# Gated linear attention and a maxout feed-forward on one core: an explicit list of steps for every engine in place of woven generators

## The chip, the core and the metric

The kernel runs on one core of one Trainium2 chip. A core has a matrix engine (TensorE, PE in the profile; its weight loads are counted apart as PEld), VectorE (DVE), ScalarE (ACT), GpSimd (POOL) and SyncE (SP), which here only starts transfers between HBM and the on-chip memory. Each engine works through its own queue in order and waits on semaphores for the others. The metric is the device time of one execution in microseconds; lower is better. A profiled span, from the first to the last instruction, is about 1 us shorter than the time.

## What is computed

The reference is a gated linear recurrence with a complex decay, followed by a feed-forward layer whose hidden value is the greatest of three products.

```python
# attention: B, H, S, D = 4, 8, 768, 48; q, k, v, a_re, a_im of that shape
mag   = sqrt(a_re**2 + a_im**2)
scale = minimum(mag, 0.999) / (mag + 1e-6)
a     = (a_re + 1j * a_im) * scale
for t in range(S):
    state = a[:, :, t, :, None] * state + k[:, :, t, :, None] * v[:, :, t, None, :]
    y[:, :, t] = q[:, :, t] @ state.real
# feed-forward: 3072 tokens, 384 channels, 768 hidden
x   = y, heads side by side           # (3072, 384)
h   = maximum(maximum(x @ w1, x @ w2), x @ w3)
out = h @ w_out
```

## The kernel before

The recurrence is done in chunks. A **tile** is 128 steps of one batch entry with all 8 heads; a **group** is a pair of tiles (two batch entries, called x and y here), and there are 12 groups. Everything is float32. For one group the work is this:

- **Gates** (the pair at once, 128 x 768): logarithm and angle of the decay, by a chain of ScalarE functions and VectorE sums. `Ln` holds minus the logarithm of the magnitude, `w` the angle in turns.
- **Sums**: TensorE adds `Ln` along time (`sums`); ScalarE takes exponentials `E` and `En`, with which key and query are multiplied. TensorE also adds the angles (`cs`), ScalarE takes sine and cosine (`CS`).
- **Tile steps**: `uk`, `uq` (key and query times sine and cosine), transposed by TensorE (`tp`) and copied by ScalarE to `K` and `Q`; decay factors between sub-chunks (`F` on TensorE, four exponentials `f` on ScalarE), with which VectorE makes further copies of query and key (three products into `Q`, and `KB`, `QB`, `QG`); scores `A` and `B` on TensorE, collected into `atm` by masked copies; state update (`dk` on TensorE, four operations on `g` by VectorE); output `y`, copied to `xT`.
- **Feed-forward**: six `up` blocks per group (18 matmul records each, 768 columns of PSUM) copied or maximised into `hT`, and one `op` block per tile, copied to `ot` and sent out.

All blocks of TensorE take their PSUM room from one pool of four buffers, in the order in which the program asks for them:

```python
psum = ctx.enter_context(tc.tile_pool(name="psum", bufs=4, space=PSUM))
def banks(nm, n=None):
    ps = psum.tile([P, 2, 512], FP, tag="ps", name=nm)
```

The weights come in as pairs of 32-bit words and are turned to float32 on the chip, in 12 blocks, each by two ScalarE and four VectorE instructions of 128 x 768:

```python
nc.scalar.activation(out=ex.bitcast(FP), in_=high.bitcast(FP), func=AF.Abs)                    # a
nc.vector.tensor_scalar(out=ex.bitcast(FP), ..., op0=OP.max, op1=OP.min)                       # b
nc.vector.tensor_single_scalar(out=ex, in_=ex, scalar=3, op=OP.logical_shift_left)             # c
nc.scalar.activation(out=dst, in_=low, func=AF.Copy, scale=2.0 ** -51, bias=2.0)               # d
nc.vector.tensor_tensor(out=ex, in0=ex, in1=dst.bitcast(I32), op=OP.add)                       # e
nc.vector.scalar_tensor_tensor(out=dst.bitcast(I32), in0=high, ..., in1=ex, ...)               # f
```

The decays of key and query, and the squares of the gates:

```python
for nm, sg in (("k", 1.0), ("q", -1.0)):
    E = nat2.tile([P, DM], FP, tag="E", name="E")
    act(out=E..., in_=ps[:, :, 0:HC], func=AF.Exp, scale=sg)
    eng = nc.gpsimd if g > 1 else nc.vector
    eng.tensor_tensor(out=hd(T[nm, x]), in0=E, in1=hd(T[nm, x]), op=OP.mult)
...
nc.scalar.activation(out=w, in_=ar, func=AF.Square)
nc.scalar.activation(out=L, in_=ai, func=AF.Square)
nc.vector._custom_dve(dve_ops.TENSOR_ADD_SAT, out=L, in0=L, in1=w, s0=LARGE, s1=SMALL)
```

The order of the program: group 0 is written out, with the weight blocks put in by hand and by `weave`, which merges several lists of steps by fractions of a common length. Groups 1 to 11 are run by `group(g)`. The program's framework may move instructions within an engine's queue as long as the data allows it. Bound are only ScalarE's functions (`tab`, because of the table loads between exponentials and sines) and, from group 2 on, TensorE's order (`chained`).

```python
weave((0.0, 1.0, tile_steps(0) + tile_steps(1)), (0.0, 0.7, rounds), (0.15, 0.58, pre_steps(1)),
      (0.415, 0.44, ffn[:6]), (0.55, 0.75, ffn[6:9]), ...)
def group(g):
    ...
    if g > 1: feed(1)                 # feed(n): the next n feed-forward blocks of the group before
    pairs(x)                          # scores A and B of tile x, and their collection
    if g > 1: gates[2]()              # last part of the gates of group g + 1
    feed(1)
    ...
    turned(y)                         # transposes, F and state of x, first query factors of y
    sums[0](); sums[1]()
    feed(1); outputs(x, tokens(x)); rest(y)
    turning()                         # angles of group g + 1; feed(2) inside
    pairs(y); ...; feed(2); turned(y + 1)
    feed(1); outputs(y, tokens(y)); rest(y + 1)
    feed(len(ffn))
for g in range(1, NG):
    if g == 2: T["chain"] = None      # TensorE's order is bound from here on
    group(g)
```

## Time and profile before

| | |
|---|---|
| time, median of 3 | 667.58 us (667.13 to 668.19) |
| profiled span | 666.7 us |
| TensorE busy | 581.8 us, 87% |
| VectorE busy | 476.9 us, 72% |
| ScalarE busy | 404.2 us, 61% |
| GpSimd busy | 122.4 us, 18% |
| TensorE clock granted, mean | 0.963 |
| instructions | 22,815 |

The page gives for every engine the time in which at least one of its instructions ran. A group line names the source line, the engine and operation, the output and inputs with their shapes and the count; after the bar stand the busy time, the mean duration of one, and the idle time of the engine just before it with what ended that idle time. Records of one engine overlap a little[...], so the step from start to start is shorter than the duration: a 128 x 768 VectorE operation shows 0.95 us and follows the last one by 0.87 us. Nearly all matmuls have the source line of one helper, so they are told apart by their tiles (`up`, `op`, `y`, `A` and so on).

### The profile page before, as it was taken

The page shows a single profiled execution, that of the slowest core. Times are in us where ns is not written, and L with a number is a line of the kernel's source. Part 1 is how long each engine was busy: PE and PEld are TensorE (multiplying, and loading weights), DVE is VectorE, ACT ScalarE, POOL GpSimd, SP SyncE. Part 2 cuts the span into 40 slices and gives each one's busy share as a digit, 9 for nine tenths or more (in the row PEclk, how much of TensorE's full clock was granted, in tenths as well). Part 3 has the DMA queues.
Part 4 walks back from the last instruction along what each step waited for, and adds up shares of the span by engine and source line. Part 5 has one row for each costly group of instructions (what it writes and reads, how often), then busy time and mean ns, then how long its engine had stood idle before and what let it go on. Part 6 is the DMA issues. An engine that isn't in the chain of part 4 may idle for free.

```text
span 666.7 us, 22815 instructions
## 1 busy us (share of the span) xinstructions
PE 581.8 (87%) x10076; PEld 472.5 (71%) x10076; DVE 476.9 (72%) x638; ACT 404.2 (61%) x670; POOL 122.4 (18%) x131
## 2 busy tenths in 40 slices
PE   1244777898999999999999999999999999999997
PEld 0143665777877878868868867878878777878785
DVE  3899998985777877877776687778778777655111
ACT  6889696577476567567566665765764854631000
POOL 9400102305113114013014013023023023000000
PEclk9956898997999999999999999999999999999999
DMA  6975542330330330330330420421320210000000
GB/s 134 272 166 142 139 83 56 62 62 14 61 65 24 61 69 19 65 69 15 73 61 15 83 52 24 76 53 35 67 56 15 40 47 3 2 27 2 19 7 24
DMA packets 136547, 39.26 MB, mean 59 GB/s; under 512 B 129152, under 2 KB 132224, under 8 KB 136448
## 3 DMA queue, kind: packets, MB, share of 16 engines
q1 hardware_dynamic: 136448, 37.80, 26.1%
q8 instruction: 79, 1.29, 0.8%
q14 instruction: 20, 0.16, 0.1%
HBM read 33.03 MB, written 4.72 MB: 57 GB/s over the span
## 4 chain that ended last, share of the span: by engine, by line
PE 46%; ACT 24%; DVE 16%; issue 8%; DMA 3%; SPq 2%; POOL 1%; DVEq 0%; POOLq 0%; ACTq 0%
PE up L117 24%; PE op L117 12%; DVE Q L533 6%; PE y L117 3%; ACT CS L112 3%; ACT f L112 2%; ACT L133 2%; ACT e L112 2%; PE A L117 2%; ACT Q L505 2%; PE cs L117 2%; ACT K L501 2%; PE dk L117 2%; DVE g L632 2%; DMA ai<-in_a_im_dram 1%
## 5 line engine op out<-in xcount | busy, mean ns | idle before, releaser
L117 PE MATMUL up<-xT,w 128*128 128x256 f32 (+1 forms) x1404 | 295.9, 369 | 11.0 <-ACT f L112 4.5
L117 PEld LDWEIGHTS up<-xT,w 128*128 128x128 f32 x1404 | 249.0, 192 | 46.9 <-ACT f L112 7.7
L533 DVE TENSOR_TENSOR Q<-Q,f 112x512 f32<-112x512 f32 (+2 forms) x72 | 91.6, 1278 | 49.2 <-ACT f L112 49.2
L117 PE MATMUL op<-wo,hT 128*128 128x384 f32 x288 | 99.0, 494 | 0.5 <-ACT K L501 0.4
L117 PEld LDWEIGHTS op<-wo,hT 128*128 128x128 f32 x288 | 53.2, 190 | 34.9 <-DVE hT L676 0.8
L674 ACT COPY hT<-up 128x768 f32<-128x768 f32 (+2 forms) x27 | 19.6, 727 | 91.8 <-PE up L117 91.7
L676 DVE TENSOR_TENSOR hT<-hT,up 128x768 f32<-128x768 f32 (+2 forms) x54 | 46.4, 859 | 38.8 <-PE up L117 38.7
L381 POOL TENSOR_TENSOR ai<-ai,L 128x768 f32<-128x768 f32 x10 | 22.3, 2226 | 276.9 <-ACT L L112 188.0
L117 PE MATMUL A<-Q,K 112*32 112x80 f32 x1536 | 34.7, 247 | 12.8 <-DVE Q L533 12.8
L117 PEld LDWEIGHTS A<-Q,K 112*32 112x32 f32 x1536 | 29.9, 117 | 21.8 <-issue 13.6
L117 PE MATMUL y<-atm,vb 128*32 128x64 f32 x1152 | 39.5, 224 | 0.9 <-issue 0.7
L117 PEld LDWEIGHTS y<-atm,vb 128*32 128x32 f32 x1152 | 32.6, 112 | 10.4 <-issue 5.6
L112 ACT ACTIVATE f<-F 48x280 f32<-48x280 f32 x96 | 38.3, 399 | 0.9
L117 PE MATMUL y<-QG,g 112*32 112x64 f32 x1408 | 38.3, 220 | 0.0
L487 DVE TENSOR_TENSOR uk<-uk,En 128x768 f32<-128x768 f32 x24 | 24.5, 1021 | 18.0 <-PE tp L117 18.0
L477 POOL TENSOR_TENSOR k<-E,k 128x384 f32<-128x384 f32 x20 | 25.6, 1279 | 63.7 <-ACT E L112 63.7
L389 POOL TENSOR_TENSOR ai<-ai,carry 1x768 f32<-1x768 f32 x10 | 18.6, 1864 | 92.8 <-ACT ai L386 92.8
L117 PE MATMUL sums<-Ln,mid 64*64 64x192 f32 x192 | 15.8, 378 | 22.7 <-DVE Ln L371 22.7
L117 PEld LDWEIGHTS y<-QG,g 112*32 112x32 f32 x1408 | 34.9, 110 | 0.4 <-ACT g L630 0.2
L477 POOL TENSOR_TENSOR q<-E,q 128x384 f32<-128x384 f32 x20 | 34.9, 1747 | 0.0
L117 PE MATMUL cs<-w,upto 128*64 128x192 f32 x192 | 20.1, 355 | 15.7 <-DVE w L400 15.7
L412 DVE SCALAR_TENSOR_TENSOR nf<-t,cs 128x384 f32<-128x384 f32 x24 | 13.3, 554 | 28.5 <-ACT t L410 27.4
(103 smaller groups left out, 949.9 us busy)
## 6 DMA issues: line engine op xcount, KB each, us to landing
ar<-in_a_re_dram SPq DMA_DIRECT2D x24, 192.0 KB
ai<-in_a_im_dram SPq DMA_DIRECT2D x24, 192.0 KB
k<-in_k_dram SPq DMA_DIRECT2D x96, 48.0 KB
q<-in_q_dram SPq DMA_DIRECT2D x96, 48.0 KB
vb<-in_v_dram SPq DMA_DIRECT2D x96, 48.0 KB
out_dram<-ot SPq DMA_DIRECT2D x24, 192.0 KB
raw<-in_moe_w_dram SPq DMA_DIRECT2D x5, 768.0 KB
w<-in_moe_w_dram SPq DMA_DIRECT2D x2, 768.0 KB
```

Source lines behind the costliest of these rows:

```text
L112: tab(nc.scalar.activation(**kw))
L117: ins = f(**kw)
L133: tab(nc.scalar.preload_act_table_set(nm))
L381: (nc.gpsimd if g > 1 else nc.vector).tensor_tensor(out=ai, in0=ai, in1=L, op=OP.mult)
L389: nc.gpsimd.tensor_tensor(out=ai[0:1], in0=ai[0:1], in1=T["carry", g], op=OP.subtract)
L477: eng.tensor_tensor(out=hd(T[nm, x]), in0=E, in1=hd(T[nm, x]), op=OP.mult)
L487: nc.vector.tensor_tensor(out=u, in0=u, in1=two(T["En", x]), op=OP.mult)
L501: nc.scalar.copy(out=T["K", x][0:DD].rearrange("p n (j t) -> p j n t", j=2), in_=src)
L505: nc.scalar.copy(out=T["Q", x][0:DD, :, 0:32].rearrange("p (n j a) t -> p j n a t", n=H, j=2), in_=src.rearrange("p j n (a t) -> p j n a t ...
L533: nc.vector.tensor_tensor(out=out, in0=in_, in1=f.to_broadcast([DD, 2 * H - g, n, 8]), op=OP.mult)
L674: nc.scalar.copy(out=dst, in_=ps)
L676: nc.vector.tensor_tensor(out=dst, in0=dst, in1=ps, op=OP.max)
```

## The change

All work is cut into single steps of about one instruction (one TensorE block, one ScalarE function, one transfer), and their order is written down in two lists. `SCHEDULE` has 472 steps: groups 0 and 1 with their weights, the feed-forward of group 0, and the first half of group 2. `CYCLE` has 143 steps and is run for g from 2 to 13: it finishes tile work of group g, prepares group g + 1, does the six `up` blocks of group g - 1 and the `op` blocks of groups g - 2 and g - 1. Every instruction of every engine is bound to the one before it, so each queue has exactly the order of the lists. It is meant to let TensorE's blocks, their emptying and the weights be placed step by step.

```diff
-    mm, mt = chained(nc.tensor.matmul), chained(nc.tensor.transpose)
+    class Bound:
+        def __getattr__(self, name):
+            f = getattr(self.engine, name)
+            def g(*a, **kw):
+                ins = f(*a, **kw)
+                if self.last is not None:
+                    tc.add_manual_dep(ins.ins, self.last.ins.name, order, reason="the schedule's order")
+                self.last = ins
+                return ins
+            return g
+    pe, dve, act, pool, sp = (Bound(e) for e in (nc.tensor, nc.vector, nc.scalar, nc.gpsimd, nc.sync))
...
-                eng = nc.gpsimd if g > 1 else nc.vector
-                eng.tensor_tensor(out=hd(T[nm, x]), in0=E, in1=hd(T[nm, x]), op=OP.mult)
+        elif name in ("mk", "mq"):
+            t = hd(T[name[1], x])
+            dve.tensor_tensor(out=t, in0=T["E" + name[1], x], in1=t, op=OP.mult)
...
-            nc.scalar.activation(out=w, in_=ar, func=AF.Square)
+            activation(out=e, in_=ar, func=AF.Square)
...
-    weave((0.0, 1.0, tile_steps(0) + tile_steps(1)), (0.0, 0.7, rounds), (0.15, 0.58, pre_steps(1)), ...)
-    for g in range(1, NG):
-        if g == 2:
-            T["chain"] = None
-        group(g)
+    program(SCHEDULE, 0)
+    for g in range(2, NG + 2):
+        program(CYCLE, g)
```

Table loads are now put in wherever the next function needs the other set, by the order of the list. The square of `a_re` goes to `e` in place of `w`. In the lists a name ends in the tile (x or y) and, after the colon, the group; `U01` is the `up` block of the first half of the hidden channels with the second weight, `u01` its maximum or copy, `O` and `o` the `op` block and its copy, `W` the weight steps a to f above, `L` a load, `D` a store. TensorE's part of `CYCLE`:

```
U00:-1 tpky:0 tpqy:0 Fy:0 U10:-1 Ax:0 Bx:0 Ox:-2 sumsx:1 sumsy:1 dkx:0 U11:-1 U01:-1 U02:-1
csy:1 csx:1 yx:0 Ay:0 By:0 U12:-1 dky:0 Fx:1 Oy:-1 yy:0 tpqx:1 tpkx:1
```

and the same stretch of VectorE's and ScalarE's part, from the first block to the second scores:

```
VectorE: mqy:0 uqy:0 Q1x:0 Q2x:0 Q3x:0 Lnop:1 KBx:0 QBx:0 addw:1 g0x:0 g1x:0 g2x:0 g3x:0 kEny:0 kEnx:0
         mkx:1 mulw:1 h0x:0 stt:1 mky:1 h1x:0 QGx:0 Q2y:0 u11:-1 h2x:0 QBy:0 mulr:1 addi:1 h3x:0
         u01:-1 Q1y:0 Q3y:0 u02:-1 nfy:1 KBy:0 ...
ScalarE: Qcx:0 expw:1 Kcx:0 relu:1 u00:-1 Kcy:0 Qcy:0 lne:1 f0y:0 f3y:0 f2y:0 abs:1 f1y:0 u10:-1 lnw:1
         b0x:0 expL:1 b1x:0 ox:-2 Ekx:1 sign:1 Eky:1 Eqx:1 Enx:1 cpai:1 Eqy:1 cpar:1 Eny:1 atan:1 ty:1
         tx:1 sby:1 afx:1 sbx:1 sax:1 xx:0 ...
```

## The prediction

> **What bounds the kernel now.** I began with the busy times in three stretches: the start, up to 151 us (where the fourth tile's output has just been copied to `xT`, at 144.85, and the second tile's result to `ot`, at 148.08), then the regular middle, then the tail. Columns after the stretch: its length, then busy us and instruction counts of TensorE, its weight loads, VectorE, ScalarE, GpSimd, the clock, DMA share, GB/s.

> ```profile
> 0.00:151.00 151.00, 86.08 (x1830) 72.42 (x1831) 128.53 (x201) 115.92 (x191) 34.42 (x78) 0.86 0.54 124
> 151.00:580.31 429.31, 413.36 (x7305) 335.30 (x7303) 322.40 (x401) 274.47 (x454) 88.00 (x53) 0.99 0.22 45
> 580.31:662.70 82.39, 82.39 (x944) 64.80 (x944) 25.99 (x36) 13.35 (x27) 0.00 (x0) 1.00 0.04 14
> 662.70:666.70 4.00, 0.01 (x1) 0.00 (x0) 0.00 (x0) 0.48 (x1) 0.00 (x0) 0.88 0.14 51
> ```

> TensorE has 581.8 us of work in a span of 666.7. Its idle time is 151.00 - 86.08 = 64.9 us in the start, 429.31 - 413.36 = 16.0 us in the middle, none in the tail, and 4.0 us at the very end (last copy and store). The start is VectorE's: 128.53 of 151 us, 85%, with ScalarE at 77%. The middle and tail are TensorE's.

> Next the middle by group. Two whole groups, same columns:

> ```profile
> 191.82:240.76 48.94, 47.21 (x853) 38.18 (x853) 37.48 (x48) 31.61 (x53) 9.89 (x6) 1.00 0.25 51
> 434.38:483.33 48.95, 47.22 (x854) 38.19 (x853) 37.49 (x48) 31.62 (x53) 9.88 (x6) 1.00 0.26 51
> ```

> A group takes 48.9 us, of which TensorE works 47.2. (Groups that lack some matmul records show less, so I take these two.) What ends its 1.7 us of idling is in the waits of TensorE between 175 and 575 us: waited for, total us, times, longest:

> ```profile
> PE dk L117 <- DVE hT L676: 5.5, 8, 0.7
> PE up L117 <- ACT f L112: 3.9, 8, 0.6
> PE up L117 <- DVE g L633: 3.6, 6, 0.6
> PE op L117 <- ACT K L501: 0.4, 1, 0.4
> ```

> None of these is data the block needs: `dk` doesn't read `hT`, and `up` reads neither `f` nor `g`. They are the four PSUM buffers: a block waits until the fourth block before it has been emptied. So 13.4 us in all are lost to late emptying.

> Last, VectorE beside GpSimd. Instructions in time order (start, duration): the query factor operations of 112 x 1024 and 112 x 768 while GpSimd rests, and then while it multiplies keys and queries:

> ```profile
> 144.10 1.22 DVE L533 TENSOR_TENSOR Q<-Q,f 112x1024 f32<-112x1024 f32 x1
> 145.70 0.95 DVE L533 TENSOR_TENSOR Q<-Q,f 112x768 f32<-112x768 f32 x1
> ...
> 162.92 1.97 DVE L533 TENSOR_TENSOR Q<-Q,f 112x1024 f32<-112x1024 f32 x1
> 164.81 1.35 DVE L632 TENSOR_TENSOR g<-g,f 112x384 f32<-112x384 f32 x1
> 166.08 1.74 DVE L533 TENSOR_TENSOR Q<-Q,f 112x768 f32<-112x768 f32 x1
> ```

> ```profile
> 163.77 1.98 POOL L477 TENSOR_TENSOR q<-E,q 128x384 f32<-128x384 f32 x1
> 165.71 1.30 POOL L477 TENSOR_TENSOR k<-E,k 128x384 f32<-128x384 f32 x1
> ```

> The same operation takes 0.95 us alone and 1.74 us beside GpSimd's products.

> [...] The trace has 25 loads of mean 1283 ns. [...]

> **The change part by part.**

> *Decays to VectorE.* From group 2 on, 4 products of 128 x 384 per group leave GpSimd (two of 1.2 us and two of 1.8 us) and come to VectorE at 0.47 us from start to start: +1.9 us per group. Against that the stretched operations return to their free length. Summing VectorE's 51 steps of `CYCLE` at free durations (14 of 0.47, 15 of 0.87, 4 maxima of 0.86, 4 of 1.13, 6 of 0.61, 2 of 0.62, 6 of 0.34) gives 34.5 us per group, against 37.5 now. VectorE has ample room in a group of 47 us; so has ScalarE, 30.0 us plus two table loads, 32.6. In the middle this part alone is worth almost nothing; its use is that the emptying comes on time.

> *The cycle.* I laid TensorE's blocks of `CYCLE` end to end (`up` 4.06 each, `op` 4.1, `y` 1.73, `A` 1.2, `dk` 1.1, others 0.5 to 0.8) and asked at each block when the fourth one before is emptied and when its data are there, going through the other two orders at free durations. Examples, in us from the start of `U00`: `U10` begins at 5.6 and needs `U00` copied, done 4.9. `Ax` (9.7) needs Q3x, done by 4.1. `sumsy` (16.4) needs A's masked copies, 12.8. `U01` (22.4) needs the three exponentials of `sumsx`, 19.3. `csy` (30.5) needs the angles, 26.7, the latest chain of gates, through GpSimd's product and carry. `Ay` (33.7) needs the maximum u02, 31.4. `yy` (45.3) needs QGy, 42.8. The next `U00` (48.1 in this sum) needs the copy of `yy`, about 47.8: two transposes of 1.1 us in all cover it. Every block has its condition ahead of time, most by over 2 us. So I expect at most 0.2 us of idling per group against 1.7: a period near 47.3 us.

> *The start.* Loads of the 472 steps at free durations: VectorE 111.6 us (weights alone 12 x (0.47 + 0.47 + 0.87 + 0.87) = 32 us) plus 3 us of memsets; TensorE 72 us; ScalarE 104.2 us plus 11 table loads by the list's alternations (1 first, 10 changes) of 1.28 = 14.1, so 118.3. Before had 7 loads up to 151 us. ScalarE is now the longest queue. It also starts late: in the chain of waits the first weight block lands at 11.2 us (3.69 + 7.53) and its first step follows, when ScalarE has done only about 6.4 us of the gates; this 4.9 us remains. The last ScalarE step needed for `yy:1`, the fourth tile's output, is at 101.4 + 10 x 1.28 of its queue, which puts the end of the list on TensorE at no earlier than 4.9 + 114.2 + 1.7 + 1.1 = 122 us. VectorE's bound is close to it (106.6 before `yy:1`, after about 10 us of waiting for the first data: 117, plus 2.8 for the last blocks). Two queues of nearly equal length that feed each other won't be without gaps. With ScalarE at 93% instead of 97% of that stretch the end is at about 128 us. That is my choice; the one stretch before ran at 77 to 85%.

> *What is left after the list.* Ten cycles of 47.2 are 472; the first lacks one `op` (-4.1), the last lacks the preparation of a next group (sums 1.6, cs 1.5, transposes 1.1, F 0.6: -4.8); then six `up` of group 11 (24.4) and three `op` (12.4): together 500 us. Before, TensorE has 413.4 + 82.4 = 495.8 us left at 151 us: the same work within its missing records, so the list's end stands for that 151.

> *Sum.* 128 + 500 + 10 x 0.2 + 0.7 (the last copy of `yy`, which no transposes cover) + 4.0 (end) + 0.9 (time over span, 667.6 - 666.7) = 635.6. I say 636 us.

> **Rivals.** (a) *The start gains nothing*: more table loads and a fixed order, in which one late transfer holds a whole queue. For it: DMA is busy 78% in the first 50 us, the weight blocks follow each other closely in the list, and SyncE's order is bound as well. Against it: the loads are written well ahead of their use in the list. Then the list ends at 151 and the time is about 659, within 2%. (b) *The cycle gets a new wait every time*, say for the angles through GpSimd or for `xT` at the seam. At 1.7 us each it would be 15 us more than I say, about 651. Against it: the slack above. (c) *VectorE becomes the bound* with 4 more products: it would need 47 us; even at its present stretched 37.5 + 1.9 = 39.4 it wouldn't be. (d) *The start is packed almost fully*, the list ends at 122: 630.

> **Range and chances.** The start is uncertain by some 7 us to either side, more to the slow side, the cycle by 0 to 8 in all, TensorE's work by 3 (clock in the start, 0.69 between 25 and 50 us, and missing records). Range 625 to 652. Over 2% faster means below 654.2, which only a failed start or a wait in every cycle would prevent: 0.90. Within 2%: 0.08. Slower: 0.02.

> **What would show it.** Right: regular periods of 47.2 to 47.5 us with TensorE waits under 0.3 us; the `xT` copy of the fourth tile at about 126 us in place of 144.85; ScalarE over 90% busy in the first 128 us, with 11 table loads; 112 x 768 query factors at a mean of 0.95 to 1.0 us in place of 1.67; only gate product and carry on GpSimd. Wrong: a wait of over 0.5 us that returns every period, or queue gaps in the start behind transfers or behind each other that put the fourth tile past 140 us.

## The result, and the profile after

The changed kernel takes 645.67 us (645.16 to 646.76, four runs) against 667.88 us (667.13 to 668.80) for the kernel before on the same chip: 0.967 of the time, with a 95% interval of 0.965 to 0.969. The profiled span went from 666.7 to 645.1 us. The prediction was 636 us in a range of 625 to 652: inside the range, and 9.7 us too low. This part follows those 9.7 us. The profiled run took 646.76 us, the slowest of the four, so its trace is some 1.1 us longer than the median run.

The stretches of the kernel after, cut where the list ends on TensorE (137.1 us) and where TensorE ends (641.5 us). Columns as in the prediction: length, busy us and counts of TensorE, weight loads, VectorE, ScalarE, GpSimd, then clock, DMA share, GB/s.

```profile
0.00:137.10 137.10, 83.38 (x1729) 70.28 (x1729) 115.56 (x193) 114.17 (x188) 31.82 (x74) 0.93 0.53 127
137.10:641.50 504.40, 495.68 (x8350) 403.02 (x8348) 359.99 (x488) 295.69 (x487) 43.34 (x17) 1.00 0.21 43
641.50:645.10 3.60, 0.01 (x1) 0.00 (x0) 0.00 (x0) 0.48 (x1) 0.00 (x0) 0.80 0.15 55
```

The opening ends at 137.1 in place of 151.0: 13.9 us gained. What is left after it takes 504.4 in place of 662.7 - 151.0 = 511.7: 7.3 us gained. The last copy and store give 0.4. So two thirds of the gain are the opening, one third is the cycle, and both were to give more.

TensorE's waits from 140 to 640 us (waited for, total us, times, longest):

```profile
PE B L129 <- issue: 4.1, 4, 1.4
PE dk L129 <- issue: 2.1, 1, 2.1
PE A L129 <- issue: 1.9, 2, 1.1
PE up L129 <- ACT xT L129: 0.6, 1, 0.6
```

The three waits for PSUM buffers that came back in every group are gone altogether. In their place stand eight single stops, 8.7 us in all; seven of them are put down to `issue`, which means that the profile shows nothing that TensorE waited for. A cycle without a stop, in the same columns, has no idle time on TensorE:

```profile
372.70:419.54 46.84, 46.84 (x856) 38.26 (x858) 37.59 (x53) 31.77 (x52) 5.99 (x2) 1.00 0.27 53
```

From copy to copy of the second tile's output the cycle takes 46.83 us in three groups and 47.5 to 48.3 us where there is a stop; it was 48.94. Group 6 takes 45.92: the two tiles there begin new batch entries (768 steps are six tiles), so half of its `y` products with a state fall away, 64 records in place of 128.

Now the opening, in steps of 25 us:

```profile
0.00:25.00 25.00, 3.15 (x80) 2.65 (x80) 12.37 (x35) 17.38 (x32) 22.03 (x71) 1.00 1.01 244
...
25.00:50.00 25.00, 8.80 (x128) 6.32 (x128) 24.15 (x37) 24.46 (x40) 0.48 (x2) 1.00 0.52 135
50.00:75.00 25.00, 15.51 (x285) 13.84 (x279) 25.00 (x37) 23.96 (x39) 2.40 (x1) 0.73 0.53 135
75.00:100.00 25.00, 21.61 (x409) 19.93 (x407) 23.29 (x37) 22.05 (x35) 6.90 (x2) 0.93 0.25 61
100.00:125.00 25.00, 24.27 (x408) 18.86 (x412) 24.09 (x39) 19.52 (x32) 0.00 (x0) 1.00 0.42 78
```

The third busy number is VectorE's: 96.5 of the 100 us after the first 25. VectorE is closer to full than ScalarE (90.0), so I take it to be what sets this stretch; but in the first 25 us it works for 12.4. The largest single cause, in the timelines of ScalarE, VectorE and GpSimd (start, duration, instruction, in brackets the idle time before it and its releaser):

```profile
19.25 0.40 ACT L129 ACTIVATE f<-F 48x280 f32<-48x280 f32 x1 [4.43 <-POOL maskf L129]
```

```profile
21.27 0.58 DVE L129 TENSOR_SCALAR ex<-ex 128x768 f32<-128x768 f32 x1 [4.35 <-ACT ex L129]
```

```profile
8.79 9.42 POOL L129 TENSOR_SCALAR_AFFINE_SELECT cuts<-cuts 64x4 f32<-64x4 f32 x32
```

GpSimd is still making the constants `cuts` until 18.2 us. The matrix `F` needs them, the first exponential `f` needs `F`, and ScalarE stands at that exponential for 4.4 us, because its queue is bound, although the next weight step `ex` (step a) needs nothing of it. VectorE waits for that `ex`. Releasers are inferred; the chain through `F` is in the code, and an experiment below undoes it.

### The profile page after: what moved, and what is told of

It reads as the page before. It is cut to its first block, busy times and chain, and to the rows that moved or that the text cites. A ratio compares the mean times of both kernels' runs of the same rounds, so it can differ in the third digit from the quotient of the medians.

```text
span 645.1 us, 22666 instructions
## 1 busy us (share of the span) xinstructions
PE 579.1 (90%) x10076; PEld 473.3 (73%) x10076; DVE 475.6 (74%) x680; ACT 410.3 (64%) x676; POOL 75.2 (12%) x91
## 3 DMA queue, kind: packets, MB, share of 16 engines
q8 instruction: 79, 1.29, 0.9%
## 4 chain that ended last, share of the span: by engine, by line
PE 82%; issue 8%; POOL 4%; ACT 2%; DMA 1%; DVE 1%; SPq 1%; POOLq 0%; ACTq 0%; DVEq 0%
PE up L129 42%; PE op L129 15%; PE y L129 6%; PE A L129 4%; PE tp L129 4%; PE dk L129 3%; PE sums L129 2%; PE cs L129 2%; PE B L129 2%; PE F L129 1%; POOL cuts L129 1%; DMA raw<-in_moe_w_dram 1%; POOL ai L129 1%; SPq L129 1%; POOL maskf L129 1%
## 5 line engine op out<-in xcount | busy, mean ns | idle before, releaser
L129 DVE TENSOR_TENSOR hT<-hT,up 128x768 f32<-128x768 f32 (+1 forms) x56 | 46.8, 836 | 52.7 <-PE up L129 52.7
L129 DVE TENSOR_TENSOR Q<-Q,f 112x512 f32<-112x512 f32 (+2 forms) x72 | 75.9, 1067 | 4.9 <-ACT Q L129 4.2
L129 ACT ACTIVATE t<-cs 128x384 f32<-128x384 f32 x24 | 11.8, 491 | 59.5 <-PE cs L129 59.5
L129 PEld LDWEIGHTS y<-atm,vb 128*32 128x32 f32 x1152 | 33.9, 114 | 17.7 <-issue 17.4
L129 PE MATMUL y<-QG,g 112*32 112x64 f32 x1408 | 39.4, 223 | 0.0
L129 ACT ACT_TABLE_LOAD x30 | 38.5, 1283 | 1.2 <-PEq L781 0.8
L129 ACT COPY ot<-op 128x384 f32<-128x384 f32 x24 | 11.5, 480 | 43.5 <-PE op L129 36.0
L129 DVE SCALAR_TENSOR_TENSOR Ln<-L,e 128x768 f32<-128x768 f32 (+1 forms) x13 | 11.7, 897 | 37.2 <-ACT e L129 36.5
L129 POOL TENSOR_TENSOR ai<-ai,carry 1x768 f32<-1x768 f32 x10 | 28.4, 2837 | 70.9 <-ACT ai L129 70.9
L129 ACT COPY atm<-B 32x256 f32<-32x256 f32 x48 | 17.3, 361 | 28.5 <-DVE atm L129 25.8
L129 ACT COPY hT<-up 128x768 f32<-128x768 f32 (+1 forms) x28 | 19.8, 708 | 23.1 <-PE up L129 20.7
L129 DVE COPY_PREDICATED atm<-maskd,A 128x512 f32<-128x512 uint8 x24 | 17.6, 734 | 22.0 <-PE A L129 22.0
```

Of the source, the lines that this page charges most:

```text
L129: ins = f(*a, **kw)
```

## The experiments

"4th `xT`" is the start of the copy of the fourth tile's output, near the list's end; "3rd" is that of the tile before. The regular cycle is the usual distance from the copy of one second tile's output to the next. Times are medians, and each ratio is to the kernel before on the same chip, with its 95% interval. Differences between two changed kernels are taken from their ratios, times 667.6 us.

| | time, us | ratio | 3rd, 4th `xT`, us | regular cycle, us |
|---|---|---|---|---|
| before | 667.88 | 1 | 123.6, 144.8 | 48.94 |
| after | 645.67 | 0.967 (0.965 to 0.969) | 127.7, 136.1 | 46.83 |
| e1_before_decay_dve | 663.18 | 0.994 (0.992 to 0.996) | 124.4, 144.7 | 48.28 |
| e2_after_decay_pool | 657.45 | 0.986 (0.983 to 0.988) | 128.1, 136.4 | 48.8 |
| e3_free_vector_pool_sync | 664.31 | 0.996 (0.994 to 0.997) | 128.3, 136.7 | 48.9 |
| e4_f_later | 642.99 | 0.964 (0.961 to 0.967) | 125.2, 133.4 | 46.83 |
| e5_v_early | 646.49 | 0.968 (0.967 to 0.970) | 128.0, 134.5 | 46.83 |
| e6_gate_product_dve | 642.72 | 0.963 (0.962 to 0.965) | 127.1, 133.6 | 46.83 |
| e7_up_between | 657.33 | 0.985 (0.983 to 0.986) | 127.1, 134.5 | 48.73 |
| e8_all | 656.32 | 0.983 (0.982 to 0.985) | 124.8, 132.1 | 48.73 |
| e9_opening | 642.07 | 0.961 (0.959 to 0.963) | 124.3, 131.8 | 46.83 |
| e10_cycle_runs | 648.09 | 0.970 (0.968 to 0.972) | 127.9, 135.4 | 47.44 |
| e11_both | 643.42 | 0.963 (0.962 to 0.965) | 125.4, 132.9 | 47.45 |
| e12_pad | 646.12 | 0.969 (0.967 to 0.971) | 128.1, 136.2 | 46.83 |

### The decays alone, done and undone

In the kernel before, the decays go to VectorE and nothing else changes:

```diff
-                eng = nc.gpsimd if g > 1 else nc.vector
+                eng = nc.vector
```

> The kernel before, with only the decay products of key and query given to VectorE for all groups; the program's order stays woven and free as it was. Theory A (the lists are what gained, the move only relieves VectorE): VectorE's 112 x 768 query factor goes from a mean of 1.67 us to about 1.0, but TensorE's PSUM waits of 1.7 us per group mostly stay; time 660 to 669 us. Theory B (the move is the gain, because VectorE no longer stands beside GpSimd): the three waits per group shrink below 0.5 us and the time falls to about 655 us or less.

The ratio of 0.9937 is 4.2 us less. TensorE's waits from 175 to 575 us, the stretch that the prediction shows of the kernel before:

```profile
PE dk L117 <- DVE hT L676: 5.5, 8, 0.7
PE up L117 <- ACT f L112: 3.9, 8, 0.6
...
```

One line of the four is gone, `up` for `g` (3.6 us); the other three have the same numbers, so most of the waiting stays, as theory A had it. The 112 x 768 factor has fallen from a mean of 1674 ns only to 1356, not to 1.0 us:

```profile
L533 DVE TENSOR_TENSOR Q<-Q,f 112x768 f32<-112x768 f32 x24 | 32.5, 1356 | 0.0
```

Its free length is 0.95 us; GpSimd's gate product and carry are left beside it. The opening doesn't move, as groups 0 and 1 had their decays on VectorE before.

The reverse, in the kernel after:

```diff
-            dve.tensor_tensor(out=t, in0=T["E" + name[1], x], in1=t, op=OP.mult)
+            (pool if g > 1 else dve).tensor_tensor(out=t, in0=T["E" + name[1], x], in1=t, op=OP.mult)
```

> The changed kernel with the decay products back on GpSimd from group 2 on, the lists as they are. Theory A (the lists rely on VectorE's free durations and on early products): the products take 1.2 to 1.8 us each on GpSimd and come later, stretched VectorE operations return, and some of the blocks that have under 2 us of slack wait; 2 to 10 us slower than the changed kernel, 648 to 656 us. Theory B (TensorE bound with ample slack, the engine of the products doesn't matter): within 1.5 us of the changed kernel.

It takes 12.4 us more than the kernel after. GpSimd's and VectorE's timelines in one cycle:

```profile
251.57 1.00 POOL L129 TENSOR_TENSOR k<-E,k 128x384 f32<-128x384 f32 x1 [38.48 <-ACT E L129]
252.53 1.81 POOL L129 TENSOR_TENSOR ai<-ai,L 128x768 f32<-128x768 f32 x1
```

```profile
254.38 1.74 DVE L129 SCALAR_TENSOR_TENSOR w<-w,ai 128x768 f32<-128x768 f32 x1 [3.61 <-POOL ai L129]
...
257.64 3.79 DVE L129 TENSOR_TENSOR Q<-Q,f 112x1024 f32<-112x1024 f32 x1
```

In a bound queue the gate product stands behind the key's product. VectorE, bound too, stands 3.6 us for it; then a 1.2 us factor is stretched to 3.8 beside GpSimd. TensorE ends up waiting for the angles (`cs`, 8.8 us in seven times from 150 us on). So the move is worth 4.2 us in the old order and 12.4 us in the new one: with a bound order a late product holds all that is queued behind it. (That it is the bond which makes the difference is read from this timeline; no run had the products on GpSimd with its order left free.)

### Which of the bonds matter

Only TensorE and ScalarE stay bound; VectorE, GpSimd and the transfers may be reordered by the framework again.

```diff
-    pe, dve, act, pool, sp = (Bound(e) for e in (nc.tensor, nc.vector, nc.scalar, nc.gpsimd, nc.sync))
+    pe, act = Bound(nc.tensor), Bound(nc.scalar)
+    dve, pool, sp = nc.vector, nc.gpsimd, nc.sync
```

> The changed kernel with the binding of the order taken off VectorE, GpSimd and SyncE; TensorE and ScalarE stay bound to the lists. Theory A (the explicit order of VectorE is needed to empty PSUM in time and to place the weights): the order chosen by the framework lets weight or gate operations go ahead of emptying, 3 to 20 us slower. Theory B (with TensorE and ScalarE bound the data alone force nearly the same order): within 2 us of the changed kernel, or faster by up to 4 us, since loads that don't wait could pass a blocked one on SyncE.

It takes 19.2 us more than the kernel after, nearly the whole gain. The 4th `xT` hardly moves (136.7), so the loss is in the cycles. TensorE waits there, from 150 to 640 us, most often for this:

```profile
PE dk L129 <- ACT atm L129: 4.9, 8, 0.6
```

`dk` doesn't read `atm`; this is a buffer once more, and the cycle is 48.9 us long. With the other waits, for `xT` above all (3.2 us in five times), the stops come to 19.2 us against 8.7, which is 10.5 of the 16.5 us by which the trace is longer. The rest is in TensorE's busy time; there are 22 stops more, and at the 0.13 to 0.22 us that a stop adds to the busy time (worked out below) I estimate 3 to 5 us for them. The order in the lists is thus needed on the emptying engines as well. In the opening TensorE's and ScalarE's order does it.

### The opening: three single moves, and together

First the exponentials that wait for GpSimd's constants, moved behind step a of weight block 2:

```diff
-... Eqx:0 Fx:0 f0x:0 Fy:0 lnw1:0 lnw0:0 Wa1:0 Wb1:0 expL0:0 mulai0:0 f3x:0 Wc1:0 ... Lrx:1 Wa2:0 sign0:0 ...
+... Eqx:0 Fx:0 Fy:0 lnw1:0 lnw0:0 Wa1:0 Wb1:0 expL0:0 mulai0:0 Wc1:0 ... Lrx:1 Wa2:0 f0x:0 f3x:0 sign0:0 ...
```

> The changed kernel with two ScalarE steps of the very beginning, the first two factor exponentials of tile x of group 0, moved seven and two places later in ScalarE's order, behind the third weight block's first step. In the changed kernel ScalarE stands 4.4 us at that place for the mask constants that GpSimd is still building (until 18.2 us), and VectorE then stands 4.35 us for ScalarE. Theory A (VectorE's late start is what sets the end of the opening list): the opening ends 3 to 4 us earlier and the time falls by 2.5 to 4 us. Theory B (the opening's end is set by its own last third, transfers and TensorE included): under 1 us.

VectorE's waits in the first 25 us: the 4.35 us are gone.

```profile
DVE Ln L129 <- ACT e L129: 2.4, 1, 2.4
...
DVE ex L129 <- ACT w L129: 1.4, 1, 1.4
```

VectorE is busy for 15.3 us of these 25 in place of 12.4, and the 3rd and 4th `xT` come 2.5 and 2.7 us earlier. So of 2.9 us more work at the start, 2.5 or more come back at the list's end. The time falls by 2.1 us by the ratios, a little less than theory A had, with intervals that overlap. The move frees ScalarE's 4.4 us too (it is busy for 19.9 of the 25 us in place of 17.4), so this run alone doesn't tell which of the two sets the end. The chain of the first gates stays (`Ln` for `e` and two more like it, 6.7 us together), which has nothing to run beside it.

Second the values of the fourth tile, loaded earlier, because a `dk` block stood 2.0 us at 128.5 us:

```diff
-Lrx:3 ... Lry:3 ... Lvx:2 ... Lvy:1
+Lvy:1 Lvx:2 Lrx:3 ... Lry:3 ...
```

> The changed kernel with the loads of v for two tiles moved ahead of one gate load in SyncE's order. That gate load waits until 116.3 us for the first output block to release its room, and the loads of v behind it wait with it; the state block of the fourth tile then stands 1.96 us. Theory A (that wait is the late load, and it is on the path): the state block doesn't wait, the copy of the fourth tile's output comes about 2 us earlier than 136.1, and the time falls by 1.5 to 2 us. Theory B (something else releases the block, or the path goes past it): under 0.7 us.

No gain: 0.9 us more by the ratios, with intervals that overlap. The load went out 7 us earlier, but `dk` still stops in the middle of its block, after 20 of 64 records. The kernel after, then this one:

```profile
130.46 0.84 PE L129 MATMUL dk<-vb,uk 64*64 64x48 f32 x44 [1.96 <-issue]
```

```profile
129.75 0.84 PE L129 MATMUL dk<-vb,uk 64*64 64x48 f32 x44 [1.02 <-issue]
```

It was not the load: e6, which leaves the loads alone, has the stop at the same record for 0.98 us. It is one of the stops in the stream of instructions that are the matter further below. The 3rd `xT` didn't move either (128.0); that the 4th comes 1.6 us earlier in this trace is this shorter stop and the TensorE clock (mean 1.00 from 127.5 to 136.0 us, 0.80 in the kernel after), of which more below.

Third the gate product of group 2, which takes 5.1 us on GpSimd, with VectorE busy for 3.4 of them:

```diff
-            (pool if g > 1 else dve).tensor_tensor(out=ai, in0=ai, in1=L, op=OP.mult)
+            (pool if g > 2 else dve).tensor_tensor(out=ai, in0=ai, in1=L, op=OP.mult)
```

> The changed kernel with one product of the gates, that of group 2 in the opening list, on VectorE in place of GpSimd. On GpSimd it took 5.1 us (87.4 to 92.5) among VectorE's two-input operations, and VectorE stood 1.7 us for it. Theory A (VectorE is the bound there, so its wait counts): VectorE does it in 0.87 us and loses no 1.7 us; 0.5 to 1.5 us faster. Theory B (0.87 us of new work on the bound engine eats the gain): within 0.5 us.

The kernel after, GpSimd and VectorE:

```profile
87.44 5.10 POOL L129 TENSOR_TENSOR ai<-ai,L 128x768 f32<-128x768 f32 x1 [22.99 <-ACT L L129]
94.49 1.80 POOL L129 TENSOR_TENSOR ai<-ai,carry 1x768 f32<-1x768 f32 x1 [1.95 <-ACT ai L129]
```

```profile
92.58 0.96 DVE L129 SCALAR_TENSOR_TENSOR w<-w,ai 128x768 f32<-128x768 f32 x1 [1.71 <-POOL ai L129]
...
94.66 2.46 DVE L129 TENSOR_TENSOR uq<-CS,q 128x768 f32<-128x768 f32 x1
```

On VectorE the product takes 0.94 us, and the 1.7 us wait goes: 0.8 us net, and the 3rd `xT` comes 0.6 us earlier, within what was expected of the move. Of the two queues it changes VectorE's alone, and nearly all of the 0.8 us comes back, which speaks for VectorE as what sets the stretch. Yet the time fell by 2.5 us by the ratios, and the trace by 3.9. The rest appears in the clock. Windows of 8.5 us around the third and fourth tile and around the first cycle's `dk` (columns as before), the kernel after and then this one:

```profile
127.50:136.00 8.50, 6.54 (x265) 5.42 (x258) 4.87 (x9) 4.51 (x10) 0.00 (x0) 0.80 0.47 108
149.50:158.00 8.50, 6.42 (x95) 5.45 (x84) 8.07 (x11) 5.65 (x11) 2.83 (x2) 0.80 0.19 32
```

```profile
127.50:136.00 8.50, 7.20 (x267) 6.14 (x258) 6.12 (x11) 6.37 (x14) 0.00 (x0) 1.00 0.37 80
149.50:158.00 8.50, 8.44 (x98) 7.58 (x99) 8.15 (x8) 6.51 (x11) 4.35 (x2) 1.00 0.28 51
```

The mean clock is 0.80 in both windows of the kernel after: each holds 3.4 us at half the clock (0.50 from 132 to 134 us and from 152.5 to 153 us), worth at most 8.5 x 0.20 = 1.7 us of full speed. Here it is 1.00. The block `dk` of 64 records shows it, after the same stop of 2.08 us in both kernels:

```profile
152.09 1.92 PE L129 MATMUL dk<-vb,uk 64*64 64x48 f32 x64 [2.08 <-issue]
```

```profile
149.56 1.14 PE L129 MATMUL dk<-vb,uk 64*64 64x48 f32 x64 [2.08 <-issue]
```

So of the gain in this trace 0.6 us is the product. The rest is clock that wasn't lost, up to 2 x 1.7, and stops of the kind described in the next section, which lie in the same stretches: the one of the fourth tile's `dk` is 1.0 us shorter, and one of 1.1 us in `A` of the first cycle isn't there. The record has only the mean clock of the timed runs: 0.980 to 0.984 in the four of the kernel after (0.980 in the profiled one), 0.986 to 0.988 here. One drop of 3.4 us to one half in 645 is 0.0026, so the means differ by fewer than two drops.

All three together:

> The changed kernel with the three changes of the opening list together: the two factor exponentials later, the loads of v earlier, the gate product of group 2 on VectorE. Alone they moved the copy of the fourth tile's output from 136.1 us to 133.4, 134.5 and 133.6. Theory A (they shorten one and the same VectorE-bound path at different places): they nearly add, the copy comes at 129 to 130.5 us and the time is 638 to 641 us. Theory B (the opening meets another limit): the copy stays at 132 or later and the time at 641 us or more.

The lowest median of all: 642.07 us, 3.8 us less than the kernel after, and those two intervals don't touch; with e4's and e6's alone it overlaps. The 3rd `xT` comes 3.4 us earlier, against 2.5 + 0.6 - 0.3 for the single moves: they add up. The 4th comes 4.3 us earlier, at 131.8, between the two theories, and the time is where theory B had it; the sum of the singles (2.7 + 1.6 + 2.5) counts the clock drop at 132 us twice, and the shorter stop of `dk` as well, which is 1.70 us here.

### The stops within the cycle

Six of the eight stops lie in the scores `A` and `B` of the second tile, which follow `y` and are followed by `up`. Two of them, in groups 3 and 5, in TensorE's timeline:

```profile
220.81 0.32 PE L129 MATMUL B<-QB,KB 112*32 112x32 f32 x8 [1.30 <-issue]
...
315.20 0.69 PE L129 MATMUL B<-QB,KB 112*32 112x32 f32 x31 [1.36 <-issue]
```

They fall inside a block (here after 24 and after 1 of its 32 matmuls), and the profile names nothing that the matmul waited for. The theory: `y`, `A` and `B` are 112 + 64 + 32 short matmuls, each with a weight load, which follow each other by some 0.02 us, and the next instructions come late. The page has a queue for instructions with 79 packets and 1.29 MB. TensorE has 20,152 matmuls and weight loads and 185 other records, so one packet holds 20,337 / 79 = 257 of them, if the queue serves that engine alone. The rival: data come late. The first test puts an `up` block (few instructions, matmuls some 0.2 us apart) between `y` and `A`:

```diff
-yx:0 Ay:0 By:0 U12:-1 dky:0
+yx:0 U12:-1 Ay:0 By:0 dky:0
```

> The changed kernel with one feed-forward block of the cycle moved from behind the scores B of tile y to between the output block of x and the scores A of y, so that the run of short matmuls (16 + 112 + 64 + 32 records in about 6 us) is cut in two. In the changed kernel 5 of 10 cycles show a gap of 0.7 to 1.4 us in the midst of A or B, with nothing in the data to wait for. Theory A (TensorE's instructions can't be brought fast enough through a long run of short ones): the gaps vanish, 3 to 5 us faster. Theory B (the gap is a late operand or buffer): A and B come 4 us later, which would remove it too, but the block moved ahead would then wait for its buffer at its new place; no gain, or 1 to 3 us slower. Gaps that stay inside a block speak against both.

The stops in `A` and `B` are gone, but the kernel takes 12.0 us more. TensorE's waits from 150 to 640 us:

```profile
PE F L129 <- DVE atm L129: 7.1, 9, 1.2
PE tp L129 <- DVE uq L129: 3.9, 8, 1.2
```

The scores come 4 us later, VectorE stands for them, and what is queued behind the collection (`uk`, `uq`, the maximum) is late in every cycle: 48.73 us. I had moved one step of one queue and not the others. e8_all has this move, the first two of the opening, and ScalarE's table for logarithms and exponentials loaded ahead of the first function.

> The changed kernel with the two factor exponentials later, the loads of v earlier, the block between the short runs, and the first function table loaded at the very start instead of after the first squares. If the single effects add: 3 to 4 us for the exponentials, 0 to 1.3 for the table, 2 for the loads of v, 3 to 5 for the block, 8 to 11 in all, 635 to 638 us. If the opening has one path that the others hide, the two parts of the opening give less than their sum.

Its opening is shorter (4th `xT` at 132.1), but the cycle is 48.73 us again, and it takes 10.8 us more than the kernel after.

The other queues are then fitted to the moved block:

```diff
-VectorE: ... nfx:1 ... g0y:0 g1y:0 g2y:0 g3y:0 ukx:1 h0y:0 u12:-1 ...
+VectorE: ... nfx:1 ukx:1 h0y:0 u12:-1 ... g0y:0 g1y:0 g2y:0 g3y:0 ...
-ScalarE: ... b1y:0 b0y:0 sqi:2 f0x:1 f2x:1 sqr:2 ...
+ScalarE: ... sqi:2 sqr:2 b1y:0 b0y:0 f0x:1 f2x:1 ...
```

> The changed kernel with the feed-forward block between the output of x and the scores A of y as before, but now with VectorE's order fitted to it: the product of key and sine, one state product and the block's maximum go ahead of the four masked copies of A, which come later now; and ScalarE's two squares go ahead of the copies of B. Theory A (the gaps came from the long run of short matmuls, and the loss with the block moved came from VectorE's and ScalarE's bound orders standing for the later A): no gaps inside A or B, the waits of F and of the query's transposes gone, period 46.9 us, time 639 to 643 us. Theory B (the place of A itself is what the cycle can't bear): the waits reappear at other blocks, 650 us or more.

That takes back most of it, 2.3 us above the kernel after: one wait stays in most cycles (`op` for `atm`, 3.1 us in six), a cycle is 47.44 us, and single `issue` stops turn up at other blocks. With the three moves of the opening:

> The changed kernel with the opening's three changes and the fitted cycle. If both theories hold and the stretches are independent, 5 to 7 us from the opening and 3 to 6 from the cycle: 633 to 638 us. If the cycle's variant fails, as much slower as that variant alone, less the opening's gain.

643.42 us: 1.4 us above e9_opening by the ratios, with intervals that overlap. In the traces nine cycles take 426.6 us against 424.5 in e9_opening (428.1 in e10 against 425.9 in the kernel after). So the given order of the cycle is the better one by some 2 us, stops and all.

The second test leaves the schedule alone and shifts TensorE's instruction stream: 64 transposes of 64 x 64 at the very start, whose result nothing reads, in the first microseconds where TensorE has nothing to do (its first block then starts at 13.25 us in place of 12.71).

```diff
+    ps = banks("pad")
+    for i in range(64):
+        pe.transpose(out=ps[0:L64, ...], in_=ident[0:L64, 0:L64], identity=ident[0:L64, 0:L64])
```

> The changed kernel with 64 extra transposes of 64 x 64 on TensorE at the very beginning, where TensorE stands until 12.7 us anyway; nobody reads their result. They add 64 matmul and 64 weight load instructions, half of one instruction packet (79 packets for 20,152 instructions, so 256 each), and move every later instruction by that much in the stream; the data, the orders and the waits stay. In the changed kernel and in two of its variants the gaps without a cause lie at the same records: in the third group's B after record 24 of 64, in the fifth group's after 1 or 2, in the ninth group's A after 48, in the tenth's B after 20, in the eleventh's after 9. Theory A (the gaps are TensorE waiting for its own instructions at packet borders): every gap moves 64 records earlier or vanishes, so B after 24 becomes A after 24, and gaps may appear in groups that had none. Theory B (the gaps come from data, buffers or other engines): the gaps stay where they are. The time changes little in both, 642 to 650 us.

None of the six stops stays at its block. There are three, in groups that had none (4 and 8 shown; the third is in group 7):

```profile
265.07 0.33 PE L129 MATMUL A<-Q,K 112*32 112x80 f32 x4 [0.91 <-issue]
...
454.22 0.51 PE L129 MATMUL B<-QB,KB 112*32 112x32 f32 x21 [1.34 <-issue]
```

The time is 1.3 us above that of the kernel after by the ratios, with intervals that overlap. In e9_opening, whose TensorE stream is that of the kernel after but runs some 6 us earlier, the six stops are at the very same records (10, 8, 31, 16, 12 and 23 before the end of their blocks), though their lengths differ (0.36 to 1.48 us). A place that goes with the stream and not with the time or the data is a property of the stream.

Counting shows which one. I number TensorE's records (matmuls, weight loads, semaphore instructions) in order of their start. The six stops of the kernel after then stand before Nos. 4544, 6336, 9665, 16,320, 18,113 and 19,648, and the three of e12 before 8128, 12,993 and 14,784: each is 192 or 193 past a multiple of 256. So is the stop of the fourth tile's `dk` (No. 3008), which the kernel after, e5 and e6 have at the same record. The trace has the times of the packets on the instruction queue too, of 16,384 bytes each. At all seven of these places of the kernel after one of them landed 1.2 to 1.6 us before TensorE went on; for No. 4544 it was under way from 169.22 to 170.60 us, and TensorE went on at 171.86. Of the 66 such borders of the kernel after from 137 us on, TensorE stops at the six where it had used the 256 instructions before in 1.95 to 2.07 us, and at none where they took 2.16 us or more. So the stops go with the place in the stream, with the packets and with the pace before them. That the row of short matmuls had used up its instructions before the next ones were at hand is my reading of these three; no record of the trace names the cause. The kernel before has no stop of this kind; there an `up` or `op` block stands between every `y` and the next `A`.

The `dk` stop of 2.08 us in the first cycle is another matter (No. 3944, 104 past a multiple of 256). It stays at the head of its block in e12, and in e4 and e6 too: VectorE ends the product of keys and `En`, for both tiles, which `dk` reads, at 151.99 us of the kernel after, and `dk` starts at 152.09. It is data.

## Why the prediction was right, and where it was not

**What held.** The mechanism held: TensorE waits for its buffers' emptying before, the order removes it, and the opening gets shorter. The three buffer waits are gone; GpSimd keeps only the gate product and the carry in the cycle; the 112 x 768 factor has a mean of 957 ns (said: 950 to 1000). VectorE doesn't become the bound of the cycle. Its work there was summed to 34.5 us and measures 37.6 to 37.9: an operation beside GpSimd's carry is still stretched (in the cycle from 232.5 us a 112 x 1024 factor takes 2.76 us from start to start in place of 1.14), and steps that don't follow at once take some 0.08 us more. Rivals (a), (c) and (d) didn't come. Rival (b), a wait in every cycle, came only when the order was disturbed (e2, e3, e7).

**The list's end: 128 said, 137.1 measured, +9.1 of the 9.7 us.** The step that failed is the ranking of the queues and the share to which they are filled. I named ScalarE the longest (118.3 us), gave VectorE 117 and said how full ScalarE would be. VectorE's load was right (114.6 summed, 115.56 busy) and ScalarE's as well (114.17), with 12 table loads where I counted 11 (the first is at 0.80 us and the next, for another set, already at 5.44). But VectorE stood 12.6 us in the first 25, where I had some 10, and from 25 to 125 us it was full (96.5%); ScalarE waited 2.8 us for it there and 6.3 us for TensorE, and was busy for 83% of the time to the list's end, not 93%. Of the first 12.6 us, 4.35 come from one bad place in the list, worth 2.5 at the 3rd `xT` (e4_f_later); the gate product on GpSimd is worth 0.6 (e6). After 125 us VectorE has work for 6.7 of 12.1 us: the last tiles' chain goes from engine to engine there, and I had allowed 2.8 us for it. 2.0 us of it is the stop of `dk` at No. 3008 and up to 1.7 the clock. These parts come to 6.8 of the 9.1 us; the rest is not told apart. Two queues of nearly equal length were given one fill factor by choice; the one I should have walked through step by step was the first 25 us of VectorE, as I had done with TensorE's cycle.

**What is left: 500 said, 495.7 busy.** I took a cycle's busy time before, 47.2, for its work; without stops it is 46.83, and the two groups at the change of batch entries are 0.9 us shorter. The 47.2 held three stops per cycle, and each stop adds some (47.21 - 46.83) / 3 = 0.13 us to the busy time too: the last matmul's record (of `A`, say, 238 ns in the mean, where the next begins some 0.02 us later) otherwise lies beside the next ones and then stands alone. The same shows in the changed kernel: the group with a 1.30 us stop takes 48.33 us, 1.50 more than 46.83, and the one with 0.83 takes 47.88, 1.05 more.

**The stalls: 2.7 us said (10 x 0.2 + 0.7), 8.7 measured.** I laid blocks end to end and asked for each block's conditions. Six of the eight stops, 6.0 us, are in no such list: they are inside blocks, at the places in the instruction stream counted above. The first cycle's `dk` (2.08) is a condition that I had checked only for a regular cycle. The seam at the end costs 0.6, as said (0.7). Busy time and stalls together come to 504.4 against 502.7: two errors that nearly cancel.

**The decays.** "In the middle this part alone is worth almost nothing" was wrong by 4.2 us (e1): I counted engine time, where TensorE paid for the lateness of `g`, whose wait of 3.6 us goes. For the new order the step was right that its use is punctual emptying, and e2 puts a number to it, 12.4 us.

**The end.** The last copy and store take 3.6 us in place of 4.0. The median time is 0.6 us above the profiled span in place of 0.9, but that term was no property of the kernel: the two profiled runs each took 1.7 us more than their spans (668.43 against 666.7, 646.76 against 645.1), and the medians lie below these runs by different amounts. Together it is 0.7 us in the other direction. 9.1 + 1.7 - 0.7 = 10.1 us above the sum of 635.6; I had rounded that to 636, which leaves 9.7.

## What to carry to other kernels

When the order of all queues is bound, one step that waits for a slow helper holds the engine and everything fed by it, so walk through the first microseconds of every queue and not only through the regular cycle; and a block can be moved in one queue only together with what empties and feeds it in the others (e7 against e10). A stop cost its idle time and a little more here (0.13 to 0.22 us), so the work in a period is to be taken from a period without stops. For a wait inside a block that the trace puts down to nothing, number the engine's instructions: if the stops stand at one place of every so many (here 256), and move to other blocks when the stream is shifted, they belong to the stream and not to the data. Then look at how fast the instructions before them went, which here were `y`, `A` and `B`, put end to end by the new order.
